# Joining two key blocks by a minimum before the transpose in a windowed attention fused with a gated MLP

## The chip, the cores and the metric

The kernel runs on one core of a Trainium2 chip. The metric is device time in microseconds (us). TensorE (PE) multiplies matrices, VectorE (DVE) and ScalarE (ACT) read and write SBUF and PSUM, GpSimd (POOL) works on SBUF here, SyncE (SP) issues most transfers. Each engine runs its own instructions in order.

## The reference

```python
B, H, S, D = 4, 8, 768, 64;  n_sink, window = 4, 128
scores = (q @ k.T) / sqrt(D)
rel = pos[:, None] - pos[None, :]
keep = (pos[None, :] < n_sink) | ((rel >= 0) & (rel < window))
scores = where(keep, scores, -1e9)
a = exp(scores - max(scores)); a = a / (sum(a) + 1e-9)
x = (a @ v).transpose(0, 2, 1, 3).reshape(3072, 512)
out = ((x @ w_a) * (x @ w_b)) @ w_out        # 512 -> 1536 -> 512
```

A row of the scores keeps the 128 keys up to its own position and the first four keys (the sinks). A tile of 128 queries therefore meets two blocks of 128 keys: its own block, of which it keeps the part up to the diagonal, and the block ahead of it, of which it keeps the rest. For each row and each column number within a block exactly one of the two blocks is kept.

## The kernel before

**Numbers.** Products are made of a rounded half ("high") and the remainder ("low") of each operand. A product in the MLP is three matmuls for each block of 128 (L800: high by high, high by low, low by high; L828: the same for the output weights). The keys lie in SBUF as `ks`, high half over low half on 128 partitions, the queries as `qh` and `ql`.

**Stages.** The first tile of each batch is done ahead of all else. After it come seven chunks of query tiles. Beside the attention of one chunk runs the MLP of the rows of the chunk ahead of it, and the steps of the attention are woven between the groups of MLP matmuls (33 slots in a stage). I call a stage by its chunk: c0 from 28 to 152.4 us of the span (another path of the code, not touched but for one small tile), c1 to 226.0, c2 to 320.7, c3 to 415.3, c4 to 509.9, c5 to 607.5, c6 to 704.0; after that the last MLP is alone. Each of c1 to c6 has 3 tiles by 8 heads, 24 units (144 in all). In c1 the MLP has 256 columns, in c2 to c6 it has 384. The chunks of c1 to c4 lie in one batch; those of c5 and c6 are a pair of tiles of one batch and a lone tile of another (two places).

**A unit before** (`scores` and `transposes` in `parts_split`). Two matmuls write the scores of 264 keys to the PSUM tile `s` (L564): 128 of the block ahead, 4 sinks in two halves (8 columns), 128 of the tile's own block. DVE adds the mask and takes the row's extremum in one custom instruction into `p` in SBUF (L569, with a short read of the accumulator). ACT takes the exponential in place with the row sum (L571), DVE makes the reciprocal (L573, L574), ACT multiplies (L575) and, for tiles from the third of a batch on, copies the sinks' columns aside (L580). Two units later PE transposes both blocks into one half of the PSUM tile `t` (L592), ACT writes the rounded half to `pt` (L595), and DVE writes the remainder, `t` less that half (L596, one operand in PSUM).

**A head before.** One unit after a head's last transposes `av` multiplies `pt` with the values (L607), ACT and DVE add up its parts (L612 to L614). Every four heads the sinks' columns are transposed (L621), split (L625) and multiplied (L634), and DVE adds the result (L636). POOL prepares the next head's keys, queries and values from their transfers: L359 rounds (one operand), L362 subtracts (two operands, both in SBUF). In the MLP ACT copies `a` to `g` (L838), DVE multiplies it by `b` (L844), ACT rounds the product (L847), POOL writes its remainder (L849). From c2 on DVE also sums up checks of the weights (L345).

**What sets the order.** A generator (`pipeline`) gives the steps of the attention: scores of unit n, transposes of unit n-2, `av` and the next head's preparation behind them. The kernel yields from it between the MLP's groups. A scheduler then arranges each engine's instructions from that program order, and buffers (`p` has 4, `s` one, `t` one in halves) add the waits.

Of the kernel before, what the change touches and what calls it, by code (L numbers as in the profile page):

```python
# [24 lines left out]
NS = 8  # L25
# [202 lines left out]
class Fast:  # L228
    def __init__(self, tc, ctx, ident, ins, out, chk):
# [7 lines left out]
        self.at = pool("f_at", 4)  # L237
# [5 lines left out]
    def consts(self):  # L243
# [287 lines left out]
    def attention(self, segs, xf, exact=False):  # L531
        tiles = [t0 + i for _, t0, n in segs for i in range(n)]
        nt = len(tiles)
        late = [i for i, t in enumerate(tiles) if t >= 2]
        parts = self.parts_exact(*segs[0], xf) if exact else self.parts_split(segs, tiles, late, xf)
        units = [(h, i) for h in range(H) for i in range(nt)]
        return self.pipeline(units, nt, late, *parts, 2, 2 if exact else 4, 1)

    def parts_split(self, segs, tiles, late, xf):
# [4 lines left out]
        units = [(h, i) for h in range(H) for i in range(nt)]  # L544
        tps, preps, state, sc, vss, skt = [], {}, {}, {}, {}, {}
# [6 lines left out]
        def do_prep(h):  # L552
            if h < H:
                preps[h] = *self.prep_kq(places, h, tag), self.prep_v(places, h, tag)
                if h % 4 == 3:
                    vss[h // 4] = self.prep_sinks(places, h // 4, tag)

        def scores(h, i):
            ks, qh, ql, vv = preps[h]
# [3 lines left out]
            for m, q in enumerate((qh, ql)):  # L563
# [6 lines left out]
                                           op0=ALU.add, op1=ALU.min, accum_out=st[:, 0:1])  # L570
            nc.scalar.activation(p[:, :w], p[:, :w], AF.Exp, bias=st[:, 0:1], scale=-1.0,  # L571
# [5 lines left out]
            if i in late:  # L577
                if h % 4 == 0:
                    sc[h // 4, i] = self.at.tile([P, 4, NS], F32, tag=f"sc{i}", name=f"sc{u}", bufs=2)
                nc.scalar.copy(sc[h // 4, i][:, h % 4, :], p[:, P:P + NS])  # L580

        def transposes(h, i):
            p = state.pop((h, i))
            u = f"{tag}_{h}_{i}"
            n = units.index((h, i))
            if not tps:
                tps.append(self.ps.tile([P, 4, P], F32, tag="t", name=f"t{u}"))
            tp = tps[0][:, 2 * (n % 2):2 * (n % 2) + 2, :]
            c1, c2, order = SLOTS[i]
            parts = {"A": p[:, :P], "B": p[:, P + NS:]}  # L590
            for k, o in enumerate(order):
                nc.tensor.transpose(tp[:, k, :], parts[o], self.ident)  # L592
            n = len(order)
            hs, ls = (self.pt_split()[:, part, c1:c1 + (n - 1) * (c2 - c1) + 1:c2 - c1, :] for part in range(2))
            nc.scalar.copy(hs, tp[:, :n, :])  # L595
            nc.vector.tensor_tensor(ls, tp[:, :n, :], hs.bitcast(F32), op=ALU.subtract)  # L596

        def av(h):
            vv = preps[h][3]
# [6 lines left out]
            for n, (blk, m, cols) in enumerate(products):  # L606
                nc.tensor.matmul(ps[:, cols], lhsT=vv[:, blk, :], rhs=m,  # L607
# [414 lines left out]
```

## Time and profile before

| | |
|---|---|
| median of 3 runs | 788.17 us (787.72 to 789.7) |
| the profiled execution | 787.82 us |
| its span, first to last instruction | 786.0 us |
| granted clock, mean | 0.998 |
| PE busy | 773.2 us (98%) |
| ACT busy | 467.1 us (59%) |
| DVE busy | 427.4 us (54%) |
| POOL busy | 341.2 us (43%) |

The span is the time on the core between the first and the last instruction; the profiled execution has 1.8 us around it. Busy shares are averages over stages with different limits. A granted clock of 1.00 in a stretch is the upper level, 2.4 GHz.

### The profile page before, as it was taken

How to read it: one execution, taken by the hardware profiler on the slowest of the kernel's cores; microseconds unless marked ns; L12 is line 12 of the kernel's file. 1: busy time of each engine (PE TensorE's matmuls, PEld its weight loads, DVE VectorE, ACT ScalarE, POOL GpSimd, SP SyncE). 2: the span in 40 equal slices, each digit the busy share in tenths (PEclk: the TensorE clock that was granted, in tenths of full speed). 3: DMA queues.
4: the chain of work that ended last, by engine and by line, in shares of the span. 5: the costliest groups of instructions: out<-in, count | busy, mean ns of one | idle time of the engine just before them, and what ended most of it. 6: DMA issues, size and time to landing. Idle time of an engine off the chain costs nothing.

```text
span 786.0 us, 13550 instructions
## 1 busy us (share of the span) xinstructions
PE 773.2 (98%) x4512; PEld 698.5 (89%) x4512; DVE 427.4 (54%) x1349; ACT 467.1 (59%) x1343; POOL 341.2 (43%) x486
## 2 busy tenths in 40 slices
PE   8999999999999999999999999999999999999997
PEld 6877777898899999999999999999999999999996
DVE  6899888566545654456544565445653456431001
ACT  6576765388646774567746777466774676631111
POOL 2200001577717545355544665357663675501110
PEclk9999999999999999999999999999999999999999
DMA  9996100412212343133331332314334142010001
GB/s 341 394 333 206 33 1 25 155 52 69 73 38 85 102 130 103 48 109 102 105 99 61 102 105 90 107 58 129 101 106 119 47 129 75 8 39 2 1 1 43
DMA packets 48875, 77.12 MB, mean 98 GB/s; under 512 B 5088, under 2 KB 28704, under 8 KB 48800
## 3 DMA queue, kind: packets, MB, share of 16 engines
q1 hardware_dynamic: 45632, 70.70, 28.1%
q10 hardware_dynamic: 3168, 5.51, 1.9%
q8 instruction: 36, 0.59, 0.3%
q14 instruction: 39, 0.32, 0.1%
HBM read 69.90 MB, written 6.29 MB: 97 GB/s over the span
## 4 chain that ended last, share of the span: by engine, by line
PE 83%; ACT 5%; DVE 4%; DMA 4%; POOL 2%; issue 1%; SPq 0%; ACTq 0%; POOLq 0%; DVEq 0%
PE o L828 23%; PE b L800 23%; PE a L800 22%; PE t L592 4%; PE s L564 4%; PE av L607 3%; ACT p L571 1%; DMA kx<-in_kD_dram 1%; PE t L723 1%; DMA v<-in_v_dram 1%; PE s L685 1%; DMA kr<-in_kT_dram 1%; ACT xf L612 1%; ACT p L575 1%; DVE pt L596 1%
## 5 line engine op out<-in xcount | busy, mean ns | idle before, releaser
L828 PE MATMUL o<-w_o,gh 128*128 128x512 f32 x576 | 186.4, 404 | 0.0
L800 PE MATMUL a<-xh,w_a 128*128 128x384 f32 (+1 forms) x672 | 183.0, 335 | 0.0
L800 PE MATMUL b<-xh,w_b 128*128 128x384 f32 (+1 forms) x672 | 181.7, 334 | 0.0
L844 DVE TENSOR_TENSOR g<-b,g 128x384 f32<-128x384 f32 (+2 forms) x96 | 53.4, 556 | 164.3 <-PE b L800 131.1
L849 POOL TENSOR_TENSOR gl<-g,gh 128x384 fp32r<-128x384 f32 (+1 forms) x70 | 68.3, 975 | 170.1 <-ACT gh L847 168.9
L800 PEld LDWEIGHTS a<-xh,w_a 128*128 128x128 f32 x672 | 120.7, 188 | 1.2
L800 PEld LDWEIGHTS b<-xh,w_b 128*128 128x128 f32 x672 | 120.3, 188 | 0.0
L828 PEld LDWEIGHTS o<-w_o,gh 128*128 128x128 f32 x576 | 103.4, 188 | 19.0 <-ACT gh L847 0.4
L828 PE MATMUL o<-w_o,gl 128*128 128x512 f32 x288 | 113.8, 395 | 0.0
L800 PE MATMUL b<-xl,w_b 128*128 128x384 f32 (+1 forms) x336 | 110.2, 328 | 0.0
L800 PE MATMUL a<-xl,w_a 128*128 128x384 f32 (+1 forms) x336 | 110.1, 328 | 0.0
L847 ACT CAST gh<-g 128x384 fp32r<-128x384 f32 (+2 forms) x96 | 49.3, 514 | 73.1 <-DVE g L844 71.3
L575 ACT ACTIVATE p<-p,st 128x264 f32<-128x264 f32 x144 | 74.0, 514 | 24.9 <-DVE st L574 24.1
L838 ACT COPY g<-a 128x384 f32<-128x384 f32 (+2 forms) x95 | 44.4, 468 | 73.8 <-PE a L800 65.1
L571 ACT ACTIVATE p<-p,st 128x264 f32<-128x264 f32 x144 | 74.3, 516 | 7.5 <-DVE st L569 7.5
L595 ACT CAST pt<-t 128x256 fp32r<-128x256 f32 x144 | 53.0, 368 | 41.8 <-PE t L592 39.9
L569 DVE CUSTOM_DVE_ANT_0 p<-s,mg 128x264 f32<-128x264 f32 x120 | 51.3, 427 | 40.7 <-PE s L564 40.5
L362 POOL TENSOR_TENSOR ks<-kr,ks 64x536 fp32r<-64x536 f32 (+1 forms) x64 | 71.5, 1124 | 4.1
L596 DVE TENSOR_TENSOR pt<-t,pt 128x256 fp32r<-128x256 f32 x144 | 60.5, 420 | 21.9 <-ACT pt L595 19.8
L828 PEld LDWEIGHTS o<-w_o,gl 128*128 128x128 f32 x288 | 54.1, 188 | 13.1
L800 PEld LDWEIGHTS a<-xl,w_a 128*128 128x128 f32 x336 | 63.3, 189 | 1.0
L800 PEld LDWEIGHTS b<-xl,w_b 128*128 128x128 f32 x336 | 63.3, 188 | 0.0
(166 smaller groups left out, 1362.2 us busy)
## 6 DMA issues: line engine op xcount, KB each, us to landing
raw_a<-in_wa_dram SPq DMA_DIRECT2D x12, 512.0 KB, 6.8
raw_b<-in_wb_dram SPq DMA_DIRECT2D x12, 512.0 KB, 7.1
raw_o<-in_wo_dram SPq DMA_DIRECT2D x12, 512.0 KB, 6.9
qr<-in_qT_dram SPq DMA_DIRECT2D x32, 192.0 KB, 2.5
chk_a<-in_wa_dram SPq DMA_DIRECT2D x24, 256.0 KB, 2.7
chk_b<-in_wb_dram SPq DMA_DIRECT2D x24, 256.0 KB, 2.6
chk_o<-in_wo_dram SPq DMA_DIRECT2D x24, 256.0 KB, 2.8
out_dram<-os ACTq DMA_DIRECT2D x21, 256.0 KB, 2.1
```

The costliest lines, as they stand in the source:

```text
L362: self.nc.gpsimd.tensor_tensor(o, i, high.bitcast(F32), op=ALU.subtract)
L569: nc.vector.tensor_tensor_reduce(out=p[:, :w], in0=ps[:, :w], in1=m, scale=-0.125, scalar=BIG, op0=ALU.add, op1=ALU.min, accum_out=st[:, 0:1])
L571: nc.scalar.activation(p[:, :w], p[:, :w], AF.Exp, bias=st[:, 0:1], scale=-1.0, accum_out=st[:, 1:2])
L575: nc.scalar.mul(p[:, :w], p[:, :w], st[:, 3:4])
L595: nc.scalar.copy(hs, tp[:, :n, :])
L596: nc.vector.tensor_tensor(ls, tp[:, :n, :], hs.bitcast(F32), op=ALU.subtract)
L800: mm = self.nc.tensor.matmul(ps[:, cols], lhsT=w[:, ksl], rhs=x[:, kk, cols], start=start and kk == 0 and i == 0, stop=kk == NK - 1 and i ...
L828: nc.tensor.matmul(outs[i], lhsT=g[:, sl], rhs=w, start=j == 0 and k == 0, stop=j == NJ - 1 and k == 2)
L838: nc.scalar.copy(g[:, :n], pa[:, :n])
L844: nc.vector.tensor_tensor(g[:, :n], pb[:, :n], g[:, :n], op=ALU.mult)
L847: nc.scalar.copy(gh[:, :n], g[:, :n])
L849: e.tensor_tensor(gl[:, :n], g[:, :n], gh[:, :n].bitcast(F32), op=ALU.subtract)
```

## The change

In the chunks c1 to c6 `flow` takes the place of `pipeline`.

- Behind the masking instruction DVE takes the minimum of the two key blocks in place: 128x128, both operands in SBUF (L614 of the new kernel). As one of the two is always masked, the minimum is the kept one. The exponential and the multiplication work on 136 columns where they worked on 264.
- A unit has one transpose where it had two. Those of a head's three tiles come in one run (L632), one step after the second score tile of the next head.
- Behind them DVE multiplies each transposed tile with two triangles of ones and zeros, `tri`, which parts the blocks again: 128x256 into `p` in SBUF, first operand in PSUM (L635). ACT rounds from there (L639), and DVE subtracts (L640). Both operands of this subtraction now lie in SBUF.
- `av` of a head comes two heads behind its scores, the values' preparation one step later than that of keys and queries, and `p` has five buffers.
- The sinks' columns are copied aside for every tile, and tile 1 of a batch goes the way of the others (masks by `late_masks`). The sinks' transposes use the PSUM tile `t`, and their split lies in the end of the `xh` tile, which is now made once.
- The slots of `pt` are numbered anew (ROW, PAIR, LONE); the matmuls of `av` keep their shapes. The chunk's steps have 7 more than the units, where they had 6.

Counts by the two orders, before and after: transposes of `p` on PE 352 and 208; sinks' transposes 30 and 36; sinks' products of 128, 256 and 384 columns 8, 20, 4 and 8, 8, 16; instructions on DVE, 144 minima and 144 triangle products more; copies of the sinks' columns on ACT 120 and 144; on POOL four more, once.

```diff
-SLOTS = ((0, 4, "BA"), (1, 2, "AB"), (3, 5, "AB"))
-ROW = ((0, 0, 2, 0), (1, 2, 2, 1), (2, 5, 0, 2), (-1, 4, 1, 0))
+ROW = ((0, 1, 2, 0), (1, 3, 2, 1), (2, 5, 0, 2), (-1, 0, 1, 0))
-        self.at = pool("f_at", 4)
+        self.at = pool("f_at", 5)
+    def triangles(self):
+        g = self.nc.gpsimd
+        g.memset(self.tri, 1.0)
+        for k, (base, step, sign) in enumerate(((-1, 1, -1), (0, -1, 1))):
+            g.affine_select(out=self.tri[:, k], in_=self.tri[:, k], compare_op=ALU.is_ge, fill=0.0,
+                            base=base, pattern=[[sign, P]], channel_multiplier=step)
+    def flow(self, nt, prepare, scores, transposes, av, sinks_t, sinks_av):
+        prepare(0, False)
+        yield
+        for h in range(H + 2):
+            for i in range(nt):
+                if h < H:
+                    scores(h, i)
+                if i == 0:
+                    if h >= 2:
+                        av(h - 2)
+                    prepare(h + 1, False)
+                    prepare(h, True)
+                elif h >= 2 and h % 4 == 1:
+                    sinks_av(h // 4 - 1, i - 1)
+                if i == 1 and 1 <= h <= H:
+                    transposes(h - 1)
+                if i == 2 and h % 4 == 0 and h:
+                    sinks_t(h // 4 - 1)
+                yield
...
+            nc.vector.tensor_tensor(p[:, :P], p[:, :P], p[:, P + NS:], op=ALU.min)
+            w = P + NS
             nc.scalar.activation(p[:, :w], p[:, :w], AF.Exp, bias=st[:, 0:1], scale=-1.0,
...
-            for k, o in enumerate(order):
-                nc.tensor.transpose(tp[:, k, :], parts[o], self.ident)
-            nc.scalar.copy(hs, tp[:, :n, :])
-            nc.vector.tensor_tensor(ls, tp[:, :n, :], hs.bitcast(F32), op=ALU.subtract)
+            units = [state.pop((h, i)) for i in range(nt)]
+            for i, p in enumerate(units):
+                nc.tensor.transpose(tp[:, i, :], p[:, :P], self.ident)
+            for i, p in enumerate(units):
+                both = p[:, :2 * P].rearrange("p (m q) -> p m q", q=P)
+                nc.vector.tensor_tensor(both, tp[:, i, :].unsqueeze(1).to_broadcast([P, 2, P]), self.tri, op=ALU.mult)
+            for i, p in enumerate(units):
+                both = p[:, :2 * P].rearrange("p (m q) -> p m q", q=P)
+                hi, lo = (pt[:, part, 2 * i:2 * i + 2, :] for part in range(2))
+                nc.scalar.copy(hi, both)
+                nc.vector.tensor_tensor(lo, both, hi.bitcast(F32), op=ALU.subtract)
```

In the order lists a name like `p_1_2_1` is that of the tile 1 of head 2 in a chunk that begins at tile 1 of its batch; the last number is the buffer's. On DVE, in stage c4 around the second score tile of a head, the order before was this:

```order
L569 ISA p_1_3_1_5581,st_1_3_1_5582<-s_1_3_1_5578,mg 128x264
L569 ISA st_1_3_1_5582 128x1
L596 TENSOR_TENSOR pt<-t_1_0_0_5254,pt 128x2x128
L573 TENSOR_SCALAR st_1_3_1_5582<-st_1_3_1_5582 128x1
L574 RECIPROCAL st_1_3_1_5582<-st_1_3_1_5582 128x1
L844 TENSOR_TENSOR g_4_5576<-b_4_5593,g_4_5576 128x384
L569 ISA p_1_3_2_5614,st_1_3_2_5615<-s_1_3_2_5611,mg 128x264
```

And this is the order of the changed kernel, on DVE in c4 between the masking instruction of the second score tile of head 2 (just ahead of the first row) and that of the third (the last row):

```order
L635 TENSOR_TENSOR p_1_1_0_5358<-t_1_5402,tri 128x256
L614 TENSOR_TENSOR p_1_2_1_5513<-p_1_2_1_5513 128x128
L635 TENSOR_TENSOR p_1_1_1_5393<-t_1_5402,tri 128x256
L635 TENSOR_TENSOR p_1_1_2_5437<-t_1_5402,tri 128x256
L618 TENSOR_SCALAR st_1_2_1_5514<-st_1_2_1_5514 128x1
L640 TENSOR_TENSOR pt<-p_1_1_0_5358,pt 128x256
L619 RECIPROCAL st_1_2_1_5514<-st_1_2_1_5514 128x1
L640 TENSOR_TENSOR pt<-p_1_1_1_5393,pt 128x256
L640 TENSOR_TENSOR pt<-p_1_1_2_5437,pt 128x256
L365 TENSOR_REDUCE chk<-chk_o_0_5415 128x1
L365 TENSOR_REDUCE chk<-chk_o_1_5417 128x1
L612 ISA p_1_2_2_5560,st_1_2_2_5561<-s_1_2_2_5557,mg 128x264
```

Where one subtraction and one product of the MLP stood between two masking instructions, there are now six instructions on 256 columns (three triangles, three subtractions, those of a whole head), a minimum and two weight checks.

On PE the changed kernel has, at the same place of c4, the three transposes of head 1 in one run behind the second scores of head 2:

```order
L607 MATMUL s_1_2_1_5510<-ks_1_2_5371,qh_1_2_5372 128x264
L607 MATMUL s_1_2_1_5510<-ks_1_2_5371,ql_1_2_5373 128x264
L632 MATMUL t_1_5402<-ident,p_1_1_0_5358 128x128
L632 MATMUL t_1_5402<-ident,p_1_1_1_5393 128x128
L632 MATMUL t_1_5402<-ident,p_1_1_2_5437 128x128
L842 MATMUL a_3_5542<-xh,w_a_698 128x384
```

Before, two transposes of the unit two steps back stood behind the scores of each unit:

```order
L564 MATMUL s_1_2_1_5434<-ks_1_2_5281,qh_1_2_5282 128x264
L564 MATMUL s_1_2_1_5434<-ks_1_2_5281,ql_1_2_5283 128x264
L592 MATMUL t_1_0_0_5254<-ident,p_1_1_2_5353 128x128 x2
L800 MATMUL a_3_5457<-xh_5127,w_a_694 128x384
L800 MATMUL a_3_5457<-xl_5128,w_a_694 128x384
```

The transposes thus wait for a multiplication that lies further back than it did, and the other two units of a head have none.

## Rows read from the trace of the kernel before

**Rows 1.** The page's busy time of each engine (share of the span, instructions).

```profile
PE 773.2 (98%) x4512; PEld 698.5 (89%) x4512; DVE 427.4 (54%) x1349; ACT 467.1 (59%) x1343; POOL 341.2 (43%) x486
```

**Rows 2.** Windows over the stages c1, c2, c4, c5 and c6: the stretch and its length, then for each engine the busy time and the number of instructions, the granted clock, the DMA share and GB/s.

```profile
core 0: us, PE busy (x) PEld busy (x) DVE busy (x) ACT busy (x) POOL busy (x), PEclk, DMA share, GB/s
...
152.40:226.00 73.60, 71.63 (x523) 65.94 (x522) 43.14 (x160) 51.82 (x163) 45.00 (x60) 1.00 0.23 67
226.00:320.70 94.70, 94.48 (x558) 88.53 (x557) 49.35 (x177) 61.29 (x188) 48.99 (x62) 1.00 0.30 93
...
415.30:509.90 94.60, 94.37 (x559) 88.46 (x558) 49.29 (x176) 61.31 (x188) 51.69 (x70) 1.00 0.31 94
509.90:607.50 97.60, 96.90 (x571) 89.84 (x570) 50.67 (x176) 62.81 (x196) 60.91 (x98) 1.00 0.34 101
607.50:704.00 96.50, 96.02 (x568) 89.04 (x567) 48.72 (x177) 58.69 (x179) 49.07 (x78) 1.00 0.19 58
```

**Rows 3.** The costliest lines of PE, the transposes' row: shapes, count, then busy time, mean ns of one, idle time ahead of them and what ended it.

```profile
L592 PE MATMUL t<-ident,p 128*128 128x128 f32 x288 | 57.0, 279 | 2.7 <-DVE pt L596 2.4
```

**Rows 4.** Timeline of PE in c3: start, duration, line, what is written and read, shapes, count. Matmuls overlap, so it is the distance of the starts that counts.

```profile
338.77 0.38 PE L592 MATMUL t<-ident,p 128*128 128x128 f32 x2
338.91 0.72 PE L828 MATMUL o<-w_o,gh 128*128 128x512 f32 x2
339.47 0.39 PE L828 MATMUL o<-w_o,gl 128*128 128x512 f32 x1
339.70 0.63 PE L828 MATMUL o<-w_o,gh 128*128 128x512 f32 x2
340.17 0.39 PE L828 MATMUL o<-w_o,gl 128*128 128x512 f32 x1
```

**Rows 5.** The lines of ACT, with the same columns: the exponential of the 264 columns, and one of 128 columns in the first tiles.

```profile
L571 ACT ACTIVATE p<-p,st 128x264 f32<-128x264 f32 x144 | 74.3, 516 | 7.5 <-DVE st L569 7.5
...
L476 ACT ACTIVATE p<-s,st 128x128 f32<-128x128 f32 x32 | 9.0, 384 | 5.1 <-DVE st L472 4.6 <-PE t L482 0.4
```

**Rows 6.** The lines of DVE, with the same columns, different shapes apart.

```profile
L596 DVE TENSOR_TENSOR pt<-t,pt 128x256 fp32r<-128x256 f32 x144 | 60.5, 420 | 21.9 <-ACT pt L595 19.8
L569 DVE CUSTOM_DVE_ANT_0 p<-s,mg 128x264 f32<-128x264 f32 x120 | 51.3, 427 | 40.7 <-PE s L564 40.5
L844 DVE TENSOR_TENSOR g<-b,g 128x384 f32<-128x384 f32 x72 | 40.1, 557 | 149.3 <-PE b L800 116.3 <-issue 27.2 <-ACT g L838 4.0
L613 DVE TENSOR_TENSOR xf<-av,xf 64x384 f32<-64x384 f32 x48 | 26.7, 555 | 21.0 <-ACT xf L612 15.6
L574 DVE RECIPROCAL st<-st 128x1 f32<-128x1 f32 x144 | 23.4, 162 | 4.1
L573 DVE TENSOR_SCALAR st<-st 128x1 f32<-128x1 f32 x144 | 21.9, 152 | 64.9 <-ACT p L571 62.8
L614 DVE TENSOR_TENSOR xf<-av,xf 64x128 f32<-64x128 f32 x48 | 13.7, 285 | 1.0
...
L345 DVE TENSOR_REDUCE chk<-chk_o 128x1 f32<-128x256 f32 x24 | 9.3, 410 | 0.6 <-DMA chk_o<-in_wo_dram 0.5
```

**Rows 7.** Timeline of DVE in c3: three neighbours that don't depend on each other's end.

```profile
330.82 0.42 DVE L569 CUSTOM_DVE_ANT_0 p<-s,m 128x264 f32<-128x264 f32 x1
331.17 0.08 DVE L569 DVE_READ_ACCUMULATOR2_ANT st<- 128x1 f32 x1
331.17 0.42 DVE L596 TENSOR_TENSOR pt<-t,pt 128x256 fp32r<-128x256 f32 x1
```

**Rows 8.** Timeline of DVE in c0, from 136.9 us on. L338 and L849 read two operands in SBUF, L844 one in PSUM and one in SBUF.

```profile
136.95 1.82 DVE L338 TENSOR_TENSOR w_a<-wf_a,w_a 128x512 fp32r<-128x512 f32 x1
138.69 0.68 DVE L844 TENSOR_TENSOR g<-b,g 128x512 f32<-128x512 f32 x1
...
139.49 1.63 DVE L338 TENSOR_TENSOR w_b<-wf_b,w_b 128x512 fp32r<-128x512 f32 x1
141.04 1.50 DVE L849 TENSOR_TENSOR gl<-g,gh 128x512 fp32r<-128x512 f32 x1
```

**Rows 9.** Timeline of DVE at 36.12 us, while POOL has no instruction.

```profile
36.12 0.69 DVE L849 TENSOR_TENSOR gl<-g,gh 128x512 fp32r<-128x512 f32 x1 [0.34 <-ACT gh L847]
```

**Rows 10.** Timeline of POOL in the stretch of rows 8.

```profile
136.57 1.65 POOL L362 TENSOR_TENSOR ks<-kr,ks 64x536 fp32r<-64x536 f32 x1
138.31 0.83 POOL L359 TENSOR_SCALAR qh<-qr 128x384 fp32r<-128x384 f32 x1
139.22 1.35 POOL L362 TENSOR_TENSOR ks<-kr,ks 64x536 fp32r<-64x536 f32 x1
140.65 1.35 POOL L362 TENSOR_TENSOR ql<-qr,qh 128x384 fp32r<-128x384 f32 x1
```

**Rows 11.** Timeline of POOL in c3: the first instruction of one head's preparation, a subtraction of it, and the first instruction of the next head's.

```profile
335.62 0.51 POOL L359 TENSOR_SCALAR qh<-qr 128x384 fp32r<-128x384 f32 x1 [1.34 <-issue]
...
336.94 1.02 POOL L362 TENSOR_TENSOR ql<-qr,qh 128x384 fp32r<-128x384 f32 x1
...
344.15 0.63 POOL L359 TENSOR_SCALAR ks<-kr 64x536 fp32r<-64x536 f32 x1 [2.48 <-PE s L564]
```

**Rows 12.** Timeline of POOL in c1: the first instruction of one head's preparation, and of the next head's.

```profile
163.37 0.51 POOL L359 TENSOR_SCALAR qh<-qr 128x384 fp32r<-128x384 f32 x1 [1.26 <-PE s L564]
...
170.02 0.51 POOL L359 TENSOR_SCALAR qh<-qr 128x384 fp32r<-128x384 f32 x1 [0.90 <-PE s L564]
```

More of the change, by code (lines that the diff above doesn't have):

```diff
@@ L263, in consts @@
         self.pt, self.kr = None, {}
+        self.tri = cp.tile([P, 2, P], BF16, name="tri")
+        self.xt = [self.mo.tile([P, NK * B * P], F32R, tag=k, name=k, bufs=1) for k in ("xh", "xl")]
         self.wt, self.raw, self.wf, self.unchecked = {}, {}, {}, []
@@ L532, in attention, with parts_split @@
         tiles = [t0 + i for _, t0, n in segs for i in range(n)]
+        if not exact:
+            return self.flow(len(tiles), *self.parts_split(segs, tiles, xf))
         nt = len(tiles)
         late = [i for i, t in enumerate(tiles) if t >= 2]
-        parts = self.parts_exact(*segs[0], xf) if exact else self.parts_split(segs, tiles, late, xf)
         units = [(h, i) for h in range(H) for i in range(nt)]
-        return self.pipeline(units, nt, late, *parts, 2, 2 if exact else 4, 1)
-    def parts_split(self, segs, tiles, late, xf):
+        return self.pipeline(units, nt, late, *self.parts_exact(*segs[0], xf), 2, 2, 1)
+    def flow(self, nt, prepare, scores, transposes, av, sinks_t, sinks_av):
[17 more added lines that the diff above has]
+                yield
+    def parts_split(self, segs, tiles, xf):
         nc = self.nc
@@ L543, in parts_split @@
         tag = f"{segs[0][0]}_{segs[0][1]}"
-        units = [(h, i) for h in range(H) for i in range(nt)]
-        tps, preps, state, sc, vss, skt = [], {}, {}, {}, {}, {}
+        tps, kq, vv, state, sc, vss, skt = [], {}, {}, {}, {}, {}, {}
         c0s = [col + i * KB for _, _, n, _, _, _, col, _, _ in places for i in range(n)]
@@ L550, in parts_split, with prepare @@
             groups = [(k + 1, *rest) for k, *rest in PAIR] + [(places[1][7] + k + 1, *rest) for k, *rest in LONE]
-        def do_prep(h):
-            if h < H:
-                preps[h] = *self.prep_kq(places, h, tag), self.prep_v(places, h, tag)
+        def prepare(h, values):
+            if not values and h < H:
+                kq[h] = self.prep_kq(places, h, tag)
+            if values and h < H:
+                vv[h] = self.prep_v(places, h, tag)
                 if h % 4 == 3:
@@ L576, in scores, with transposes @@
             state[h, i] = p
[L577 to L585, printed above, removed]
-            if not tps:
[L587 to L590, printed above, removed]
-            for k, o in enumerate(order):
-                nc.tensor.transpose(tp[:, k, :], parts[o], self.ident)
-            n = len(order)
-            hs, ls = (self.pt_split()[:, part, c1:c1 + (n - 1) * (c2 - c1) + 1:c2 - c1, :] for part in range(2))
-            nc.scalar.copy(hs, tp[:, :n, :])
-            nc.vector.tensor_tensor(ls, tp[:, :n, :], hs.bitcast(F32), op=ALU.subtract)
+            if h % 4 == 0:
+                sc[h // 4, i] = self.at.tile([P, 4, NS], F32, tag=f"sc{i}", name=f"sc{u}", bufs=2)
+            nc.scalar.copy(sc[h // 4, i][:, h % 4, :], p[:, P:w])
+        def transposes(h):
+            if not tps:
+                tps.append(self.ps.tile([P, 4, P], F32, tag="t", name=f"t{tag}"))
+            tp, pt = tps[0], self.pt_split()
+            units = [state.pop((h, i)) for i in range(nt)]
[9 more added lines that the diff above has]
+                nc.vector.tensor_tensor(lo, both, hi.bitcast(F32), op=ALU.subtract)
         def av(h):
-            vv = preps[h][3]
             ps = self.ps.tile([P, 4 * P], F32, tag="av", name=f"av{tag}_{h}")
@@ L896, in run @@
         self.verdict = lambda gp: verdict(val, gp)
-        xs = tuple(self.new_x(B, "first"))
+        xs = self.new_x(B)
         self.in_order = True
@@ L904, in run @@
         self.in_order = False
+        self.triangles()
         rows = [b * S for b in range(B)]
```

64 lines of the change are left out of this document (37 added, 27 removed).

## Prediction

> **What bounds the kernel now.** I read the busy times first: PE is busy for 773.2 of the span's 786.0 us, the others for 43 to 59% of it [rows 1]. So the time can fall by work taken off PE, if nothing else begins to hold PE up. Then the windows by stage [rows 2]: in each of c1 to c6 PE is idle for almost nothing, 1.97 us in c1, 0.2 in each of c2 to c4, 0.70 in c5, 0.48 in c6, 3.8 us in all. The granted clock is 1.00 in every one, the upper level, so no part of the time hangs on it. DVE is busy for 59% of c1 and 52% of c4, POOL for 61% of c1, 55% of c4 and 62% of c5. These shares are low enough that DVE and POOL don't hold PE up today; the question is whether that stays so.
>
> **What is removed.** 144 transposes on PE. A transpose is recorded at 279 ns [rows 3], but that is its latency in a pipeline. In the timeline [rows 4] two transposes start at 338.77 and the next matmul at 338.91, 0.14 later; the two MLP matmuls behind take 0.56 to the next start where the same pair otherwise takes 0.47 (339.70 to 340.17). So a pair of transposes takes 0.14 + 0.09 = 0.23 of PE, one 0.115. I take 0.1125, so 144 x 0.1125 = 16.2 us.
> The Trainium skill's page "TensorE: Matmul & The Clock Gate", Part 4, gives about 275 ns for a 128x128 transpose within a kernel. The recorded duration agrees with 279 ns, but the distances of the starts don't: by the page's figure the saving would be 39.6 us, and I don't take it.
> Against this stand six more transposes of the sinks' columns, 6 x 0.115 = 0.7 us, and twelve of their products with 128 columns more; 512 columns take 0.23 (339.47 to 339.70), 128 thus 0.058, 0.7 us in all. PE's work falls by **14.8 us**. The rest of PE's instructions stay.
> ACT saves too: the exponential and the multiplication at 264 columns take 0.516 each, one of 128 took 0.384 [rows 5]; 24 more small copies are little against that. ACT was at 59% and isn't what ends the waits, so I count nothing. The set-up of triangles and masks is a handful of small instructions of POOL and DVE beside c0's MLP: nothing, at most 1 us if it is late at a stage's head.
>
> **What is added on DVE.** Per unit a minimum of 128x128 (nearest row: 64x128, 0.285) and a triangle product of 128x256 (nearest row: the subtraction of that shape with one operand in PSUM, 0.420) [rows 6]. Neighbours that don't depend on each other overlap by some 0.07: the first ends at 331.24, the next two begin at 331.17 [rows 7]. The two add some 0.21 + 0.35 = 0.56 a unit, 81 us over 144 units. None of it costs anything while DVE keeps ahead of PE.
> The subtraction keeps its shape, but both its operands now lie in SBUF, as do the minimum's: 288 such instructions, six a head.
>
> **What that does beside POOL.** Such instructions and POOL's are seen together in c0. While POOL works, DVE's 128x512 instructions with two operands in SBUF take 1.82, 1.63 and 1.50 us [rows 8], against 0.69 when POOL is quiet [rows 9]. Each ends 0.55 behind the end of a POOL instruction (138.22 and 138.77, 140.57 and 141.12, 142.00 and 142.54 [rows 8, 10]): it stands until POOL's instruction is through. L844, with one operand in PSUM, takes 0.68 in the same stretch, so the triangles and the masks should not wait. POOL pays as well: a subtraction of queries takes 1.35 behind such a wait [rows 10], and 1.02 in c3 [rows 11].
> The Trainium skill's page "SBUF — State Buffer", section "Who interferes with whom", says that a DVE instruction with two SBUF inputs contends with a GpSimd one that reads SBUF, as an exclusive lock. The rows above agree with it; it is the rule that speaks against this change.
> The price of one wait: in c1 POOL is busy for 61% with a mean instruction of 45.0/60 = 0.75 [rows 2], so an instruction that comes at any moment waits 0.61 x 0.375 = 0.23, six of them 1.4 us a head. In c2 to c4 it is about 0.2, 1.2 a head. The bounds are 0 (they fall into POOL's gaps) and a wait of 0.5 for each, 3.0 a head.
>
> **c1.** A head takes 6.65 us, from one preparation to the next [rows 12]. Less three transposes (0.34) and today's idle time of 1.97/8, PE alone needs 6.06. DVE needs in that time [rows 6] three units of mask 0.43 + 0.08, minimum 0.29, sum 0.15, reciprocal 0.16, so 3.33; three triangles and three subtractions 2.52; the two additions of a head's result 0.84; about one product of the MLP 0.42 (256 columns); the sinks some 0.2: 7.3, less 23 overlaps of 0.07, 5.7. With 1.4 of waits 7.1, over PE's 6.06. Some of the waits fall where DVE would stand for ACT or PE anyway, so I take 0.7 a head, 5.5 us, between 0 and 8.
>
> **c2 to c4.** A head takes 8.53 [rows 11], about 8.2 afterwards, and DVE's sum has room on the average. But the order crowds six instructions and a minimum between the masks of a head's second and third score tile. There is one score bank, so the third mask must have read it ahead of the first scores of the next head. From the end of the second scores that is three transposes 0.34, two groups of twelve matmuls of 384 columns (0.175 each by rows 4, so 2.1), and scores 0.24: 4.8 us. On DVE stand mask 0.51, three triangles 1.26, minimum 0.29, sum and reciprocal 0.31, three subtractions 1.26, two weight checks 0.82, then the third mask 0.43: 4.9, less eleven overlaps, 4.1; with four waits of 0.2, 4.9. That is just the cover: some heads stall by a few tenths. I take 1 us a stage, 3 in all, between 0 and 7.5.
>
> **c5 and c6.** The same with more POOL instructions (98 in c5 [rows 2]) and one product more in `av`: 0.3 a head, 2.5 us each, 5 in all, between 0 and 10.
>
> **What goes.** Two transposes stood behind each unit's scores and waited for that unit's ACT work of two units ago; now three stand at one place, further behind it. I let today's 3.8 us of idle go whole; what is late next is the score bank, priced above.
>
> **The sum**, against the profiled execution's own 787.82: - 14.8 - 3.8 + 5.5 + 3 + 5 = 782.7. The median of the runs lies 0.35 above that execution, so **783**.
>
> **The rivals.**
> - *The cover holds* everywhere: the waits fall into gaps, as POOL's work comes in bursts behind each head's last scores and rests after (0.90 us in c1 [rows 12], 2.48 in c3 [rows 11]). Then only PE's work counts: 787.8 - 14.8 = 773, from 770 to 777. For it: DVE at 50 to 59%. Against it: c1, where the rest is short.
> - *DVE with the port becomes the bound*, slower than before: if each of the six instructions waits some 0.5, DVE needs 5.7 + 3.0 = 8.7 in a head of c1 (over by 2.6, 21 us), and some 0.2 to 0.4 a head in each other stage (8 to 16 us). It decides from 18.6 us of new stalls in all, 0.39 a head over 48 heads. The time would be 791 to 800. For it: in c0 each such instruction seen beside a busy POOL waited. Against it: POOL's gaps, and masks that don't wait.
> - *A wash*: stalls of 16 to 21 us, no change within 2.4 us. It is the middle between my sum and the last.
> - *The change doesn't do what it says*: the transposes gone were idle time's cover and PE waits for ACT at the same places. Against it: PE is busy for 98%, and the waits at the transposes are 2.7 us in all [rows 3]. I give it nothing of its own.
>
> **How the numbers follow.** A partial gain (777.5 to 785.5): 0.42. The cover holds (770 to 777.5): 0.20. A wash: 0.18. Slower: 0.20. A measurement of this kernel can tell about 0.3%, 2.4 us, from no change; by that faster has 0.62, within it 0.18, slower 0.20. The range leaves out the last part of the gain and of the loss, about one in ten each: 772 to 793, and the likeliest case's own is 777.5 to 785.5.
>
> **What would show it.** In the profile after: PE busy falls by some 15 us in c1 to c6 (right) or not (wrong). PE's idle time in c1 is the largest of the stages, some 5 us, ended by DVE's masks or, behind them, the score bank; under a microsecond there is the second case. The minimum and the subtraction have means well above 0.29 and 0.42, while the triangle keeps 0.42: that is the wait for POOL; at 0.29 and 0.42 the price was nothing. POOL's instructions are longer where DVE's stand beside them. I am wrong if the idle time stands ahead of `av` or the transposes instead (a chain of DVE, ACT and DVE that comes late), or if the scores wait for POOL's preparation.

## The result

The changed kernel took **797.61 us** (median of 4 runs, 796.27 to 798.11) against 788.62 of the kernel before on the same chip: ratio 1.0111, 95% interval 1.0091 to 1.013. It is slower by 1.1%, outside the range of 772 to 793. The profiled execution has a span of 794.6 us at a granted clock of 1.00.

The busy times of the page after, answering to [rows 1]:

```profile
PE 765.6 (96%) x4374; PEld 689.7 (87%) x4374; DVE 544.1 (68%) x1640; ACT 454.5 (57%) x1367; POOL 349.2 (44%) x490
```

PE is busy for 7.6 us less and DVE for 117 us more. The chain that ended last shows where the span went instead (share of the span by engine; the kernel before in the first row, the kernel after in the second):

```profile
PE 83%; ACT 5%; DVE 4%; DMA 4%; POOL 2%; issue 1%; SPq 0%; ACTq 0%; POOLq 0%; DVEq 0%
...
PE 70%; DVE 14%; POOL 5%; issue 3%; ACT 3%; DMA 3%; SPq 1%; POOLq 0%; ACTq 0%; DVEq 0%
```

Below are windows of the kernel after, each from the first scores of a chunk to the first scores of the next, c1 to c5, answering to [rows 2]:

```profile
156.00:240.90 84.90, 72.80 (x501) 65.92 (x500) 68.73 (x208) 48.46 (x162) 48.15 (x62) 1.00 0.19 56
240.90:334.90 94.00, 93.03 (x535) 86.70 (x534) 68.92 (x224) 60.03 (x195) 49.84 (x62) 1.00 0.31 97
334.90:428.80 93.90, 92.92 (x536) 86.92 (x535) 67.81 (x224) 59.79 (x195) 49.70 (x62) 1.00 0.31 97
428.80:522.10 93.30, 92.61 (x537) 86.98 (x536) 67.04 (x224) 59.99 (x195) 52.07 (x70) 1.00 0.31 97
522.10:620.80 98.70, 95.50 (x547) 87.90 (x547) 68.30 (x224) 59.88 (x195) 62.01 (x98) 1.00 0.33 100
```

By the same marks the kernel before took 75.1, 94.5, 94.6, 94.6 and 97.6 us. So the loss is in c1: 9.8 us more, with PE idle for 12.1 of its 84.9 us. c2 to c4 are shorter by 0.5 to 1.3 each, and c5 is longer by 1.1.

The lines of DVE that the prediction spoke of, in c1 alone:

```profile
L640 DVE TENSOR_TENSOR pt<-p,pt 128x256 fp32r<-128x256 f32 x24 | 18.8, 816 | 0.0
L614 DVE TENSOR_TENSOR p<-p 128x128 f32<-128x128 f32 x24 | 13.0, 542 | 0.4
...
L635 DVE TENSOR_TENSOR p<-t,tri 128x256 f32<-128x256 f32 x24 | 9.2, 414 | 1.1 <-PE t L632 1.1
```

The triangles keep their price of 0.41. The subtraction, the same shape, takes 0.816 in the mean, and the minimum 0.542. And the waits of PE in c1 (engine and line, what it waited for, us in total, times, longest):

```profile
PE s L607 <- DVE st L612: 5.8, 5, 2.9
PE av L650 <- DVE pt L640: 3.1, 3, 2.2
PE sk L676 <- ACT g L880: 1.5, 1, 1.5
PE t L632 <- ACT p L620: 1.4, 2, 0.8
```

The score bank, whose mask comes late on DVE, and `av`, whose subtraction comes late, make up most of it. Here is the longest of them. DVE's timeline first:

```profile
172.96 0.64 DVE L640 TENSOR_TENSOR pt<-p,pt 128x256 fp32r<-128x256 f32 x1
173.51 0.15 DVE L619 RECIPROCAL st<-st 128x1 f32<-128x1 f32 x1
173.59 3.19 DVE L640 TENSOR_TENSOR pt<-p,pt 128x256 fp32r<-128x256 f32 x2
176.71 0.42 DVE L612 CUSTOM_DVE_ANT_0 p<-s,mg 128x264 f32<-128x264 f32 x1
```

POOL's in the same stretch:

```profile
172.81 0.51 POOL L379 TENSOR_SCALAR qh<-qr 128x384 fp32r<-128x384 f32 x1 [1.92 <-PE s L607]
173.29 0.80 POOL L379 TENSOR_SCALAR ks<-kr 64x536 fp32r<-64x536 f32 x1
174.06 0.99 POOL L382 TENSOR_TENSOR ql<-qr,qh 128x384 fp32r<-128x384 f32 x1
175.12 1.38 POOL L382 TENSOR_TENSOR ks<-kr,ks 64x536 fp32r<-64x536 f32 x1
```

And PE's:

```profile
174.11 0.28 PE L650 MATMUL av<-pt,vv 128*128 128x256 f32 x1
177.28 0.36 PE L607 MATMUL s<-ks,qh 128*128 128x264 f32 x1 [2.89 <-DVE st L612]
```

A head's last scores let POOL begin the next preparation at 172.81, and the three subtractions of the head before it come from 172.96 on. The first ends at 173.60, 0.28 behind the end of POOL's rounding of the queries (173.32). The last two take 3.19 us where two of 0.41 would do; they end at 176.78, 0.28 behind the end of POOL's subtraction of the keys (176.50). The mask of the next tile stands behind them on DVE, and the next scores stand behind that mask: 2.89 us of PE.

### The profile page after: what moved, and what is told of

Read it like the earlier page. It is cut to its first block, busy times and chain, and to the rows that moved or that the text cites. A ratio compares the mean times of both kernels' runs of the same rounds, so it can differ in the third digit from the quotient of the medians.

```text
span 794.6 us, 13660 instructions
## 1 busy us (share of the span) xinstructions
PE 765.6 (96%) x4374; PEld 689.7 (87%) x4374; DVE 544.1 (68%) x1640; ACT 454.5 (57%) x1367; POOL 349.2 (44%) x490
## 4 chain that ended last, share of the span: by engine, by line
PE 70%; DVE 14%; POOL 5%; issue 3%; ACT 3%; DMA 3%; SPq 1%; POOLq 0%; ACTq 0%; DVEq 0%
PE o L870 20%; PE b L842 20%; PE a L842 19%; DVE pt L640 3%; PE av L650 3%; PE s L607 3%; DVE p L614 3%; DVE p L635 2%; DVE p L612 2%; ACT p L616 1%; POOL ks L382 1%; DMA kx<-in_kD_dram 1%; PE t L632 1%; PE t L765 1%; DMA v<-in_v_dram 1%
## 5 line engine op out<-in xcount | busy, mean ns | idle before, releaser
L842 PE MATMUL a<-xh,w_a 128*128 128x384 f32 (+2 forms) x760 | 214.8, 344 | 0.0
L842 PE MATMUL b<-xh,w_b 128*128 128x384 f32 (+2 forms) x768 | 214.6, 342 | 0.0
L842 PEld LDWEIGHTS b<-xh,w_b 128*128 128x128 f32 x768 | 139.6, 188 | 4.2
L842 PE MATMUL b<-xl,w_b 128*128 128x384 f32 (+2 forms) x384 | 129.8, 338 | 0.0
L842 PE MATMUL a<-xl,w_a 128*128 128x384 f32 (+2 forms) x380 | 128.4, 338 | 0.0
L616 ACT ACTIVATE p<-p,st 128x136 f32<-128x136 f32 x144 | 58.7, 408 | 49.0 <-DVE p L614 41.2
L640 DVE TENSOR_TENSOR pt<-p,pt 128x256 fp32r<-128x256 f32 x144 | 74.0, 548 | 2.6 <-ACT pt L639 2.6
L382 POOL TENSOR_TENSOR ks<-kr,ks 64x536 fp32r<-64x536 f32 (+2 forms) x64 | 72.1, 1132 | 4.3
L620 ACT ACTIVATE p<-p,st 128x136 f32<-128x136 f32 x144 | 58.6, 407 | 24.3 <-DVE st L619 21.3
L614 DVE TENSOR_TENSOR p<-p 128x128 f32<-128x128 f32 x144 | 69.6, 483 | 2.2
L639 ACT CAST pt<-p 128x256 fp32r<-128x256 f32 x144 | 52.4, 401 | 18.8 <-DVE p L635 18.4
```

The source lines that it names most:

```text
L382: self.nc.gpsimd.tensor_tensor(o, i, high.bitcast(F32), op=ALU.subtract)
L614: nc.vector.tensor_tensor(p[:, :P], p[:, :P], p[:, P + NS:], op=ALU.min)
L620: nc.scalar.mul(p[:, :w], p[:, :w], st[:, 3:4])
L639: nc.scalar.copy(hi, both)
L640: nc.vector.tensor_tensor(lo, both, hi.bitcast(F32), op=ALU.subtract)
L842: mm = self.nc.tensor.matmul(ps[:, cols], lhsT=w[:, ksl], rhs=x[:, kk, cols], start=start and kk == 0 and i == 0, stop=kk == NK - 1 and i ...
```

## The experiments

All are timed beside runs of the kernel before on the same chip (its medians there: 788.20, 787.92 and 788.32 us). Stage lengths are those of the one profiled execution of each kernel, from the first scores of a chunk to those of the next, as above; the times are medians. The granted clock, a mean over the stage, is 1.00 in these stages, but 0.96 in c1 of the minimum from PSUM, and 0.98 in c5 of the subtraction, of both and of v1, in c1 of v3, in c2 of o1, and in c2 and c3 of x2.

| kernel | us | c1 | c2 | c3 | c4 | c5 |
|---|---|---|---|---|---|---|
| before | 788.6 | 75.1 | 94.5 | 94.6 | 94.6 | 97.6 |
| after | 797.6 | 84.9 | 94.0 | 93.9 | 93.3 | 98.7 |
| subtraction from PSUM | 790.1 | 76.1 | 92.9 | 93.5 | 92.9 | 101.6 |
| minimum from PSUM | 794.1 | 83.0 | 93.3 | 93.1 | 93.9 | 98.0 |
| both from PSUM | 786.1 | 74.3 | 92.5 | 93.1 | 92.9 | 100.6 |
| order only | 784.2 | 69.9 | 93.5 | 93.4 | 93.4 | 101.1 |
| POOL without its subtractions | 780.2 | 76.2 | 93.4 | 93.6 | 93.4 | 94.5 |
| v1, low half through PSUM | 793.7 | 77.5 | 95.4 | 94.5 | 95.8 | 99.7 |
| v2, sinks in the score bank | 792.3 | 77.6 | 95.3 | 95.3 | 96.4 | 97.5 |
| v3, keys asked for earlier | 793.5 | 79.2 | 95.8 | 95.7 | 95.0 | 97.9 |
| o1, order only, checks moved | 781.7 | 70.0 | 97.4 | 95.8 | 94.8 | 93.7 |
| x1, rounding on ACT | 806.7 | 80.0 | 96.1 | 96.7 | 97.2 | 102.8 |
| x2, v1 in c1, checks moved | 800.3 | 77.3 | 99.9 | 99.9 | 97.5 | 95.0 |
| x3, x2 and x1 | 794.3 | 76.2 | 96.7 | 96.6 | 99.8 | 94.4 |

The theory was that DVE's instructions with two operands in SBUF wait for POOL (port). Its rivals were that DVE simply has too much to do (work), and that the new order of the steps makes PE wait (order).

**Subtraction from PSUM.**

```diff
-                nc.vector.tensor_tensor(lo, both, hi.bitcast(F32), op=ALU.subtract)
+                nc.vector.tensor_tensor(lo, tp[:, i, :].unsqueeze(1).to_broadcast([P, 2, P]), hi.bitcast(F32), op=ALU.subtract)
```

> The changed kernel with one operand changed: the subtraction that makes the low half reads the transposed tile in PSUM (both blocks from the same 128 columns) where it read the triangle product in SBUF. Same count, shape and place; the low half is that of the unparted tile, so that part of the output is not the reference's. Theory port (DVE's instructions with two operands in SBUF stand until POOL's running instruction ends, and the score bank and av wait behind them): the subtraction's mean falls from 548 to about 420 ns, and of c1's some 12 us of PE idle time more than half goes; 780 to 787 us. Theory work (DVE simply has too much to do, the waits only fill its idle time): 795 to 799. Theory order (three transposes in one run and av two heads late are the cause): 795 to 799.

Measured: 790.14 us, ratio 1.0022 (1.0003 to 1.0042), 7.5 less than after; c1 8.8 us less. The forecast of the port was 780 to 787: the direction is the port's, the size smaller. Part of it is lost again in c5, which is 2.9 us longer than in the changed kernel, at a granted clock of 0.98. The line in this kernel:

```profile
L640 DVE TENSOR_TENSOR pt<-t,pt 128x256 fp32r<-128x256 f32 x144 | 53.8, 410 | 3.2 <-ACT pt L639 3.2
```

In the changed kernel, whole, it was this, with the minimum behind it:

```profile
L640 DVE TENSOR_TENSOR pt<-p,pt 128x256 fp32r<-128x256 f32 x144 | 74.0, 548 | 2.6 <-ACT pt L639 2.6
L614 DVE TENSOR_TENSOR p<-p 128x128 f32<-128x128 f32 x144 | 69.6, 483 | 2.2
```

One operand's place takes the subtraction's mean from 548 to 410 ns.

**Minimum from PSUM.**

```diff
-            nc.vector.tensor_tensor(p[:, :P], p[:, :P], p[:, P + NS:], op=ALU.min)
+            nc.vector.tensor_tensor(p[:, :P], ps[:, P + NS:], p[:, :P], op=ALU.min)
```

> The changed kernel with one operand of the minimum read from the score bank in PSUM (the block's raw scores) where it was read from SBUF. Same count and shape; the score bank is held some 0.3 us longer; the minimum is taken against unmasked scores, so the output is not the reference's. Theory port: the minimum's mean falls from 483 to about 290 ns, PE's idle time falls less than in the first run, since in c1 the minima wait 6 us and the subtractions 10; 786 to 792 us. Theories work and order: 795 to 800.

Measured: 794.13 us, ratio 1.0082 (1.0055 to 1.0109), 3.5 less than after. It lies between the port's forecast (786 to 792) and that of its rivals (795 to 800). The minimum's mean falls from 483 to 287 ns, as the port has it. c1 falls by only 1.9 us, but at a granted clock of 0.96 there; PE's idle time in c1 falls by 5.1 us, from 12.1 to 7.0.

**Both from PSUM.** Both lines above. 

> Both edits of the first two runs together, so that no instruction that the change added or altered has two operands in SBUF; the output is not the reference's, as there. Theory port: nearly the whole gain of the transposes that went is seen, 772 to 778 us, and PE's idle time in c1 is under 3 us. Theory work: the instructions are all still there, so 793 or more. Theory order: 793 or more.

Measured: 786.14 us, ratio 0.9987 (0.9977 to 0.9998). The two gains add up: the port costs the changed kernel some 11.5 us. The two lines now:

```profile
L640 DVE TENSOR_TENSOR pt<-t,pt 128x256 fp32r<-128x256 f32 x144 | 54.3, 412 | 5.1 <-ACT pt L639 4.1
...
L614 DVE TENSOR_TENSOR p<-s,p 128x128 f32<-128x128 f32 x144 | 41.2, 286 | 2.1
```

But neither theory had it whole: the port's forecast of 772 to 778 is missed by 8 us, so something else takes most of what the transposes gave. The rows of c1 and c5 (columns of [rows 2]):

```profile
155.50:229.80 74.30, 70.81 (x501) 65.48 (x500) 52.45 (x208) 47.35 (x162) 46.07 (x62) 1.00 0.21 65
508.30:608.90 100.60, 96.20 (x549) 89.53 (x548) 61.92 (x224) 59.83 (x195) 60.84 (x98) 0.98 0.32 98
```

c1 has lost most of its trouble: PE is idle for 3.5 us there. Of these, 1.4 belong to the edit, since scores wait for the minimum, which now reads the score bank. c5 is longer than in the kernel before, in part at a granted clock of 0.98.

**Order only.**

```diff
-            nc.vector.tensor_tensor(p[:, :P], p[:, :P], p[:, P + NS:], op=ALU.min)
...
-                nc.vector.tensor_tensor(both, tp[:, i, :].unsqueeze(1).to_broadcast([P, 2, P]), self.tri, op=ALU.mult)
...
-                both = p[:, :2 * P].rearrange("p (m q) -> p m q", q=P)
+                both = tp[:, i, :].unsqueeze(1).to_broadcast([P, 2, P])
```

> The new order of the steps alone: neither minimum nor triangles, ACT's rounding and DVE's subtraction read the transposed tile in PSUM; what is left out is the joining and the parting of the two blocks, so the output is not the reference's. Theory order: PE still waits at the transposes, av and scores, 785 or more. Theories port and work: the full gain of 14.8 us and today's idle time, 769 to 775 us.

Measured: 784.20 us, ratio 0.996 (0.9946 to 0.9974). Neither forecast holds (785 or more, 769 to 775), but it lies at the edge of that of the order. Without the minima and the triangles the new order gives 4 us in place of some 18.6. c1 is near what the sum wanted (75.1 less 2.7 of transposes and 2.0 of idle time, 70.4):

```profile
156.80:226.70 69.90, 69.38 (x500) 65.38 (x499) 42.61 (x160) 47.91 (x162) 46.16 (x62) 1.00 0.22 69
```

But c5 is 101.1, and each of c2 to c4 gives only 1.1. Over the whole kernel PE's waits name POOL and the sinks' transposes: 2.8 and 1.5 us of scores on L382 and L379, 2.3 of the output products on L887's remainder, 3.6 at the sinks' transposes, which now use the bank `t`, on DVE's subtractions. PE's longest waits in c5 are all for POOL:

```profile
PE o L866 <- POOL gl L887: 2.3, 1, 2.3
PE s L607 <- POOL ql L382: 1.4, 2, 0.7
PE s L607 <- POOL qh L379: 1.3, 2, 1.0
```

POOL itself waits in c5 (507 to 608 us) for transfers:

```profile
POOL qh L379 <- DMA qr<-in_qT_dram: 5.4, 4, 2.1
POOL ks L379 <- DMA kr<-in_kT_dram: 5.4, 2, 4.0
POOL gl L887 <- DMA kr<-in_kT_dram: 5.0, 1, 5.0
...
POOL vv L379 <- DMA vr<-in_vB_dram: 2.1, 2, 1.5
```

An MLP remainder (`gl`) stands behind a transfer of keys in POOL's queue. But POOL waited for the keys' and queries' transfers in the c5 of the kernel before as well, where PE was idle for only 0.7 us:

```profile
POOL ks L359 <- DMA kr<-in_kT_dram: 7.4, 3, 4.6
POOL qh L359 <- DMA qr<-in_qT_dram: 4.5, 4, 2.0
```

**POOL without its subtractions.**

```diff
     def rest(self, o, i, high):
-        self.nc.gpsimd.tensor_tensor(o, i, high.bitcast(F32), op=ALU.subtract)
+        self.nc.gpsimd.memset(o.bitcast(F32), 0.0)
```

> The changed kernel, with POOL's subtractions in the preparation of keys, queries and values (L382) replaced by a memset of the same region: POOL then has no two-operand instruction there and reads SBUF far less; the low halves of those operands are left out (zeros), so the output is not the reference's. DVE's instructions are untouched. Theory port: the minimum and the subtraction fall to some 0.32 and 0.45 us in the mean, PE's idle time in c1 falls to a few us, and the waits of c5 for queries that come late from POOL go too: 778 to 785 us. Rival (DVE's two-operand instructions are slow for another reason than POOL, or DVE's amount of work is the cause): 794 or more.

Measured: 780.24 us, ratio 0.991 (0.9888 to 0.9931). DVE's program is untouched, and its lines change all the same:

```profile
L640 DVE TENSOR_TENSOR pt<-p,pt 128x256 fp32r<-128x256 f32 x144 | 63.0, 473 | 2.0 <-ACT pt L639 2.0
L614 DVE TENSOR_TENSOR p<-p 128x128 f32<-128x128 f32 x144 | 50.6, 351 | 2.2
```

They were 548 and 483 ns. So it is POOL's instructions that hold them up. And as soon as POOL is lighter, c5 is 94.5 us, where the sum wanted 94.2 (97.6 less 2.7 and 0.7), and the stretch from c6's first scores to the end is 171.4, where it wanted 171.3 (174.5 less 2.7 and 0.5).

**v1, v2, v3: the same function by other means.** v1 takes the low half before the parting:

```diff
+            nc.scalar.copy(f3, t3)
+            nc.vector.tensor_tensor(hi, wide, tri, op=ALU.mult)
+            nc.vector.tensor_tensor(t3, t3, f3.bitcast(F32), op=ALU.subtract)
+            nc.vector.tensor_tensor(lo, wide, tri, op=ALU.mult)
```

> The changed kernel with the parting in another way, the same function: ACT rounds the three unparted tiles at once, DVE multiplies the transposed tiles by the triangles straight into the high half, subtracts the rounded tiles in place in PSUM, and multiplies the remainder by the triangles into the low half. Four DVE instructions a head of up to 768 columns with one operand in PSUM each, where there were six; the minimum still has both operands in SBUF. Theory port: as the first run (790 us) within 3, since only the minima wait: 786 to 791. If what counts is the amount of DVE's work, the columns are about the same: 795 or more.

v2 moves the sinks back to the score bank:

```diff
-            tp = tps[0][:q, :nt, :]
+            tp = self.ps.tile([q, 3 * P], F32, tag="s", name=f"skt{tag}_{g}").rearrange("p (c q) -> p c q", q=P)[:, :nt, :]
```

> The kernel of v1 with the sinks' transposes in the score bank s, as in the kernel before, where the change put them into the bank of the transposes t. The order-only run waited 3.6 us at these transposes for DVE's subtractions. Theory order-by-banks: 2 to 4 us less than v1, and the wait at L664 goes. Rival: the wait moves to the next scores, whose bank is then held: within 1 us of v1.

v3 asks for keys and queries a step earlier:

```diff
-                    prepare(h + 1, False)
                     prepare(h, True)
...
+                if i == 2:
+                    prepare(h + 2, False)
```

> The kernel of v2 with the preparation of keys and queries asked for one step earlier in the program. In c5 PE waits for queries that POOL makes late, and POOL there waits for transfers. If the late call is the cause: 2 to 5 us less than v2, and c5 back to some 97 us. Rival: the cause is the ring of six transfer buffers, which the values now hold a head longer: within 1 us of v2, and c5 still over 100 us.

Measured: 793.65 (1.0044 to 1.0089), 792.29 (1.0046 to 1.0094), 793.48 us (1.0049 to 1.0086). v1 gets c1 down to 77.5, near the 76.1 of the subtraction from PSUM, and misses its forecast by 3 us: c2 to c4 are 0.6 to 2.5 us longer each than in the changed kernel. One instruction of 768 columns takes 0.95 us on DVE there; that this is the reason isn't shown. v2 is 1.4 less, between its two forecasts and within what these runs can tell. PE's waits at the sinks' transposes fall from 1.1 to 0.2 us, and those of `av` for DVE's L643 rise from 0.4 to 1.8. v3 gains nothing over v2. It tells nothing of c5, which was under 98 us already in v2.

**o1: order only, checks moved off c5.**

```diff
-                k = (c - 2) * 8 + j - 2
-                if c >= 2 and 2 <= j < 10 and k < len(order):
+                k = (c - 2) * NJ + j
+                if 2 <= c < 5 and k < len(order):
```

> The order-only kernel (neither minimum nor triangles: the joining and the parting of the blocks are left out), with the weight checks of c5 and c6 moved to c2 to c4, twelve a stage. Their transfers share the ring of six buffers with the keys, queries and values. In the order-only run c5 took 101.1 us (97.6 before), and PE waited there for queries and remainders that POOL made late. Theory ring (values read a head later hold the ring's buffers, and the loads behind come late): c5 falls to 95 to 97 us, c2 to c4 stay within 0.5 each, 778 to 781 us. Rival (POOL itself has too much to do in c5): c5 stays over 100 and the time within 1 us of 784.

Measured: 781.68 us, ratio 0.9919 (0.9894 to 0.9944). c5 falls from 101.1 to 93.7, and POOL's waits for the queries' and keys' transfers there are gone (515 to 609 us):

```profile
POOL qh L379 <- PE s L607: 6.6, 3, 3.9
POOL gl L887 <- ACT gh L885: 5.0, 2, 3.3
POOL vs L379 <- DMA vsr<-in_vS_dram: 2.2, 1, 2.2
POOL vv L379 <- PE av L646: 1.2, 1, 1.2
```

That is the ring's direction for c5, and more than its forecast of 95 to 97. c2 to c4 were to stay within 0.5 and rose by 3.9, 2.4 and 1.4, the first of them at a granted clock of 0.98: four more checks a stage cost as much there as c5 gave. What the kernel gained as a whole lies behind c6's first scores (171.2 us from there to the end, against 173.7), where the last of the checks had been. So the time missed its 778 to 781 by a little. The checks' work on DVE and ACT left c5 and c6 too; these runs don't part it from the ring's share.

**x1, x2, x3: the same function, for a gain.** x1 replaces POOL's rounding instruction:

```diff
-        self.nc.gpsimd.tensor_scalar(o, i, 1.0, 1.0, op0=ALU.mult, op1=ALU.mult)
+        self.nc.scalar.copy(o, i)
```

> The changed kernel with the rounding of keys, queries and values (L379) on ACT in place of POOL, the same function. POOL's busy time falls from 349 to some 255 us, ACT's rises from 455 to some 530. Theory port: DVE's two-operand instructions meet POOL less often; the minimum's and the subtraction's means fall by a third of their excess, PE's idle time in c1 by some 4 us, and c5 loses its waits: 788 to 793 us. Rival (ACT, in whose queue the roundings now stand before exponentials, becomes late): 797 or more.

x2 uses v1's four lines where `self.short` holds, which is set in c1 alone, and o1's place of the checks.

```diff
+            if self.short:
+                nc.scalar.copy(f3, t3)
...
+                self.short = c == 1
```

> The changed kernel, the same function, with two edits: in c1 alone the parting as in v1 (one operand of each DVE instruction in PSUM), and the weight checks moved to c2 to c4. Theory: c1 falls from 84.9 to some 77.5 us as in v1, c5 from 98.7 to some 96; c2 to c4, where the checks are three a head instead of two, within 0.5 of 94 each: 786 to 789 us. If the checks crowd DVE in c2 to c4: 790 or more.

> The kernel of x2 with the roundings on ACT as in x1. Theory port: 780 to 786 us, under the kernel before. Rival (ACT late): 788 or more.

Measured: 806.68 (1.0197 to 1.0261), 800.34 (1.0127 to 1.0206) and 794.25 us (1.0059 to 1.0118). In x1 c1 falls by 4.9 as the port has it, but c2 to c4 rise by 2.1 to 3.9 each and c5 by 4.1, and PE waits for ACT's roundings (2.1 us at L379): the rival won. In x2 c1 came out as forecast (77.3, 77.5 foreseen), and c5 at 95.0 (96), but with twelve checks a stage beside the crowded DVE each of c2 to c4 is 4 to 6 us longer, part of it at a granted clock of 0.98 in c2 and c3. x3 misses its 780 to 786 as well, with c2 to c4 still 2.7 to 6.5 us longer than in the changed kernel: the rival again. No version of the whole function tried here beats the kernel before.

## Why the prediction was wrong, point by point

**What PE saves: right.** In c3 of the kernel after three transposes start at 342.48 and the next matmul at 342.73:

```profile
342.48 0.49 PE L632 MATMUL t<-ident,p 128*128 128x128 f32 x3
342.73 0.42 PE L842 MATMUL a<-xh,w_a 128*128 128x384 f32 x1
342.99 0.34 PE L842 MATMUL a<-xl,w_a 128*128 128x384 f32 x1
```

That is 0.25, and 0.09 more to the start behind where 0.17 is usual: 0.34 for three, the 0.1125 each of the sum. Order-only's c1, 69.9 us, is within 0.5 of the 75.1 of before less 24 x 0.1125 and less 2.0 of idle time (70.4). The page's busy time was a poor sign: it falls by 7.6 us in place of some 15, in part because an instruction behind a wait is recorded longer (the scores at 177.28 have 0.36 where 0.28 is usual). Where PE hardly waits, its busy time holds with the sum: 69.4 us in c1 of order-only and 93.5 in c5 of o1, where 73.1 and 97.0 before, less 2.7, give 70.4 and 94.3.

**c1: the step that failed.** "I take 0.7 a head, 5.5 us, between 0 and 8." c1 took 84.9 against those 70.4: 14.5 us, 1.8 a head. So this term is 9.0 us too small, of the 13.7 by which all the stalls of the sum are (13.5 there; 27.2 by the spans, 794.6 less 786.0 and 18.6 more). Three things in that paragraph were off.
- The price of a wait, "an instruction that comes at any moment waits 0.61 x 0.375 = 0.23". The instructions don't come at any moment. The end of a head's last scores frees POOL's buffers, and the three subtractions of the head before come just then: in seven of c1's eight heads POOL begins within 0.7 us of the first of them. 16 of c1's 24 subtractions end 0.27 to 0.29 us behind the end of a POOL instruction, and two of these stood through two of POOL's. In the last head POOL has no preparation to do, and its three subtractions take 0.41 to 0.42 each. Against the 0.412 and 0.286 of both-from-PSUM the waits in c1 are 24 x (0.816 - 0.412) = 9.7 and 24 x (0.542 - 0.286) = 6.1 us, 2.0 a head in place of 1.4.
- "Some of the waits fall where DVE would stand for ACT or PE anyway": I took half of them. At most a third did: taking the port away gives c1 10.6 us of those 15.8 (84.9 to 74.3).
- The work without waits was held to fit, 5.7 in 6.06. It costs 4.4 us in c1 (74.3 against 69.9), of which 1.4 is the wait for the minimum that reads the score bank in that run. That some head is always late with so little room is my reading.

My own bound, a wait of 0.5 or 3.0 a head, would have given 2.6 a head in c1, over the measured 1.8; I used it for the rival and not for the upper end of the term. That rival, DVE with the port as the bound, 791 to 800, has the time that came, at 0.20. In part that is luck: it drew its time from the port alone, with 21 us in c1, where the port costs 11.5 in all, and the order of the steps, which it left out, costs more.

**c2 to c4: too small, cause mixed.** The sum wants 92.1 us in each: 94.6 less 2.7 and 0.2 of idle time, and 0.5 more for the sinks' added transposes and products, which all fall in these three stages. They took 94.0, 93.9 and 93.3, which is 4.9 in place of 3, within the term's 0 to 7.5. The stall that I put at the score bank is there, 1.0 us in c2 and 0.6 in each of c3 and c4 by PE's waits on DVE's mask. But order-only has c2 to c4 nearly as long (93.5, 93.4, 93.4) without any of DVE's new work, 1.3 each over the sum. So most of what is missing there comes from the order. PE's one wait in these stages of order-only is at the sinks' transposes in the bank `t`, 0.8 to 0.9 us each; the rest is small pieces that I can't name. I had let the order's cost at nothing beyond the score bank.

**c5: sum too small, cause in part open.** c5 took 98.7, 4.5 over 97.6 less 2.7 and 0.7 of idle time, where I had 2.5. The cause is not mainly the port: both-from-PSUM has 100.6 there, and order-only 101.1 at the full clock. POOL is late: it ends 5.0 of PE's 5.8 us of idle time in order-only's c5, and a lighter POOL brings c5 to 94.5. In the changed kernel itself POOL's queries end 1.6 us of PE's waits in c5, and DVE ends 1.7. Why POOL is late is not shown. My reading is that values read a head later hold the ring of six transfer buffers longer, so that keys and queries come late. For it: in order-only's c5 SP, which issues the transfers in order, stands 17.3 us ahead of the queries' transfers for POOL's subtraction of values, 8.7 before. Against it: POOL's own waits for keys and queries in c5 are 9.6 us in the changed kernel and 11.9 in the kernel before. No run puts the values back in their place, which would settle it. I had listed the move of the values' preparation and not followed its transfers through SP's queue. c6 came as summed: from its first scores to the end 173.8 us, 2.5 over 174.5 less 2.7 and 0.5 of idle time.

**The account.** Of a full gain of 18.6 us (14.8 of work, 3.8 of idle time) from 788.2, the order alone leaves 4 us; DVE's work without waits takes 2 of them (786.1 against 784.2), the port 11.5 (797.6 against 786.1), and the sign turns. The order's part is the larger, 14.6 us: about half of it is c5 (101.1 against 94.2), some 4 are c2 to c4 (93.4 against 92.1 each), 2.4 lie behind c6's first scores (173.7 against 171.3), and 1.7 in a later beginning of c1, which differs by as much from run to run. These parts don't simply add up stage by stage: in c5 the changed kernel loses 4.5 us, and order-only 6.9.

## What to carry to other kernels

An estimate of waiting from busy shares holds only if the two engines' work is not set off by the same event; look up what starts each burst, and if both hang on one instruction, let the term's range reach to the price of the bound. Here a head's six waits came to 2.0 us, between the 1.4 of the shares and the 3.0 of the bound. When a step is moved later, follow what it holds, transfer buffers too, and who stands in the queue behind. Where one stage leaves an engine little room (here 5.7 of 6.1 us a head), its share of the span says little; give that stage a range with its own upper bound.

## What the runs showed of the hardware

The way the two engines share was sharper than I had it. A subtraction of 256 columns ends 0.28 us behind POOL's instruction (176.50 and 176.78), as those of 512 columns ended 0.55 behind theirs [rows 8, 10], and 12 of c1's 24 minima of 128 columns end 0.15 behind one: the columns run only once POOL is through. They don't strictly take turns: the second subtraction above, begun at 173.59, let a rest of the keys' rounding (to 174.09) and the whole subtraction of the queries (174.06 to 175.05) go by and ended at 175.33. The loss is nearly all on DVE's side here: POOL's busy time is 349.2 us in the kernel after and 341.2 before [rows 1], 2% more, while DVE's 288 instructions took 48 us more than their kinds did with an operand in PSUM (144 x (0.548 - 0.410) + 144 x (0.483 - 0.286)).
